# Routing of a sticky mixture of experts: packed keys, a triangle product and a carry product in place of VectorE steps, and a new order for the last tiles

## The chip, the cores and the metric

One Trainium2 chip, one core. The time is the device time of one execution in microseconds; lower is better. The engines are named as in the profile: PE is TensorE (PEld its weight loads), DVE is VectorE, ACT is ScalarE, POOL is GpSimd, SP is SyncE, whose queue issues most of the DMAs.

## The reference, cut to what matters

Three layers follow each other on 768 tokens of 512 columns: an attention in which a query sees only keys of its own hash bucket, a gated feed-forward layer with a 768 by 768 mixing of tokens (w_sg) and an output projection, and a mixture of 8 experts. The change lies in the choice of the expert in the third:

```python
logits = np.einsum('bsd,de->bse', x, w_gate)         # 768 x 8
local_gate = 1.0 / (1.0 + np.exp(-np.einsum('bsd,de->bse', x, w_local).squeeze(-1)))
prev_e = -1
for s in range(S):
    fresh_e = int(np.argmax(logits[b, s]))
    if s == 0 or local_gate[b, s] < 0.5:
        e = fresh_e
    else:
        e = prev_e if prev_e >= 0 else fresh_e
    prev_e = e
    p = softmax(logits[b, s])
    h = np.maximum(x[b, s] @ w1[e], 0.0)
    out[b, s] = p[e] * (h @ w2[e])
```

(The softmax and the loop's indices are abridged.) The choice is sticky: a token whose local gate is at or above one half takes the expert of the last token before it whose gate was below. It is thus a running "last update" over 768 tokens, then a count of how many tokens each expert has got so far.

## The kernel before, in words

Tokens are in 6 tiles of 128, one token per partition. The work runs in three stages: attention (8 heads), feed-forward with mixing, experts. In the second and third the order of the work is written out by hand: a text such as MIXING names one step after another ("mix 3 4", "out 5 6", "route 4", "gx 2 1"), the kernel records them in that order, and each engine executes its own instructions in the order in which they were recorded. An instruction that waits holds up all that stands behind it on its engine.

For each tile t of 128 tokens in MIXING: 18 products "mix" (PE, tile vs, 512 columns wide), the gating (DVE, g), 4 transposes (PE, gT), their rounding on ACT (gh) and the rest on DVE (gl), 12 products "out" (PE, tile o), the residual on DVE (x, L772). Then the routing of that tile, the generator route(t), whose steps are the "route t" of the text:

- 4 transposes of x (PE, x2T), a copy (ACT, x2t), the 9 logits (PE, lg): for tiles 0 to 4 in 32-wide column groups and a summing product, for tile 5 directly.
- DVE: the maximum of the 8 logits (rmx), whether the token updates (upd), the code of the maximal expert (sel, rw), the key of the token (key, L821): 8 times its position plus the code, or zero. ACT: the exponentials (ex, into the PSUM bank route_bank) with their sum se.
- PE transposes the key, spread over 128 columns (route_bank, L824; the last tile has a bank of its own, pk); DVE masks it with a triangle (km), takes the row maximum (pm), and the maximum with the tiles before (carry). Four DVE steps get the code out of the key (rf), two make the 8-wide choice in two types (ohb_all, oh_all).
- PE counts: products of the earlier tiles' choices with a matrix of ones, and of this tile's with a triangle (rk). DVE takes out the token's rank and its place (d), writes a 128 by 256 selection (pick, L863), a 128 by 128 one (slot, in gbc or cst), and ids and probabilities (what_all).

The selections are used at once: "gx" products gather the rows of the first two experts on PE out of the halves x2h (ACT) and x2l (POOL) of x, 8 products of 256 columns for each tile, and "fill" products gather the table of ids and probabilities. When the gx of tile 5 are done, the first expert's products (eh) start. In the expert stage PE multiplies by weights that arrive in 64 DMAs of 512 KB (raw, issued by SP); each is cast by ACT (w, L657) and its rest is formed by DVE or POOL (w, L663), which frees the buffer for the next DMA.

iota_p and rev_p (constants), the exponentials and the keys' product all lie in the one tile route_bank, and a reader or writer of any part of it waits for the last writer or readers of the tile.

Of the kernel before, what the change touches and what calls it, by code (L numbers as in the profile page):

```python
# [120 lines left out]
route 1, out 2 7, mix 4 10, gT 3, route 0, route 1, mix 4 11, route 1, out 2 8, out 2 9, wr 0, wh 0, wsg 5 1, wl 0,
mix 5 2, mix 4 12, route 1 *4, out 2 10, out 3 0, out 2 11, mix 4 13, res 2, route 1 *3, xd 2, mix 4 14,
route 1 *2, mix 5 3, wh 0, out 3 1, route 1, route 2, route 1, mix 4 15, out 3 2, wr 0, out 3 3, mix 4 16, out 3 4,
route 1, mix 4 17, out 3 5, wl 0, gated 4, mix 5 4, out 3 6, route 2, gl 3, mix 5 5, gT 4, mix 5 6, out 3 7,
out 3 8, route 2, out 3 9, route 1, out 3 10, out 3 11, wr 0, mix 5 7, route 1, mix 5 8, mix 5 9, route 2,
half 2 0, route 2 *2, out 4 0, mix 5 10, res 3, route 2 *2, mix 5 11, mix 5 12, mix 5 13, out 4 1, gl 4, route 2,
wh 0, route 2, mix 5 14, route 2, wr 0, out 4 2, mix 5 15, route 2, wh 0, mix 5 16, out 4 3, route 2, mix 5 17,
out 4 4, route 3, gated 5, route 2 *3, out 4 5, xd 0, route 2 *2, out 4 6, gT 5, route 2 *2, wl 0, route 3,
out 4 7, gl 5, out 5 0, wh 0, xd 1, out 4 8, route 3, out 4 9, route 3, out 4 10, route 2, out 4 11, out 5 1,
out 5 2, route 3, route 2, half 1 1, wl 0, half 2 1, route 3, res 4, route 3 *2, out 5 3, route 3 *3, out 5 4,  # L130
out 5 5, route 3, out 5 6, route 4, route 3, wr 0, out 5 7, out 5 8, route 3 *2, out 5 9, out 5 10, out 5 11,
route 3, res 5, xd 3, xd 5, route 3, wh 0, route 3, wr 0, route 3, xd 4, route 3, route 4, route 3, route 5,
route 4, route 5, route 4, route 3, gx 0 1, gx 0 0, gx 0 3, route 4 *2, half 4 0, half 5 0, route 5 *2, gx 1 0,
route 4, wl 0, half 3 0, route 5 *2, half 3 1, half 4 1, half 5 1, route 4, gx 0 2, route 4, wh 0, wr 0, route 4,
gx 1 1, fill 0, gx 1 3, route 4 *2, gx 1 2, route 5 *2, gx 2 1, gx 2 3, route 4 *3, wl 0, fill 1, gx 2 0, gx 2 2,
# [1121 lines left out]
```

## Time and profile before

| | before |
|---|---|
| median of 3 runs | 339.02 us (338.87 to 339.11) |
| the profiled execution | 338.87 us |
| its span | 336.9 us |
| PE busy | 325.5 us (97%), 1860 instructions |
| DVE busy | 264.8 us (79%), 504 instructions |
| ACT busy | 234.8 us (70%) |
| POOL busy | 203.9 us (61%) |

The span is what the profile shows of the core; 2.0 us of the execution's own time lie around it. Busy shares are of the span. Products on PE are pipelined: an entry lasts longer than the distance to the next one, so the distance between starts is what an instruction takes of PE's time.

### The profile page before, as it was taken

What the parts mean: (1) busy time and instruction counts of PE and PEld (TensorE: products, weight loads), DVE (VectorE), ACT (ScalarE), POOL (GpSimd) and SP (SyncE); (2) the same over time, 40 slices, a digit from 0 to 9 for tenths busy, and PEclk for the clock granted to TensorE, in tenths of its full rate; (3) what the DMA queues carried; (4) which work ended last, traced back from release to release, by engine and by line L of the source; (5) the groups of instructions that cost most, each with busy time, mean ns of one, the idle gap of its engine ahead of it and who ended that gap; (6) DMA issues with size and microseconds to landing.
All of it is one profiled execution on the core that took longest, in us unless ns stands there. A gap on an engine that the chain in (4) does not pass through costs nothing. (4 is left out here: it accounts for less than half of the span.)

```text
span 336.9 us, 5434 instructions
## 1 busy us (share of the span) xinstructions
PE 325.5 (97%) x1860; PEld 255.0 (76%) x1860; DVE 264.8 (79%) x504; ACT 234.8 (70%) x433; POOL 203.9 (61%) x162
## 2 busy tenths in 40 slices
PE   7899999999999999999999999999999999999994
PEld 6787786677678677688878777778878888788883
DVE  4899999998998884878864557888569877798970
ACT  3589888887988776288663455466659785978651
POOL 3378868587967745245734575949732683564652
PEclk9999999999999999999999999999999999999999
DMA  6914042214240115003014537456979979999711
GB/s 254 341 43 157 3 156 68 102 52 158 67 154 8 56 63 140 2 0 110 11 38 173 177 104 206 171 202 253 339 287 347 325 280 400 324 342 364 259 48 47
DMA packets 25952, 55.82 MB, mean 166 GB/s; under 512 B 2879, under 2 KB 7487, under 8 KB 25921
## 3 DMA queue, kind: packets, MB, share of 16 engines
q1 hardware_dynamic: 23872, 50.67, 42.7%
q0 software_dynamic: 1120, 3.15, 2.6%
q10 hardware_dynamic: 928, 1.62, 1.4%
q8 instruction: 16, 0.26, 0.3%
q14 instruction: 16, 0.12, 0.1%
HBM read 52.28 MB, written 3.67 MB: 166 GB/s over the span
## 5 line engine op out<-in xcount | busy, mean ns | idle before, releaser
L663 POOL TENSOR_TENSOR w<-raw,w 128x1024 fp32r<-128x1024 f32 x23 | 59.1, 2573 | 39.1 <-ACT w L657 38.0
L657 ACT CAST w<-raw 128x1024 fp32r<-128x1024 f32 x64 | 65.7, 1055 | 11.7 <-DMA raw<-in_w 9.2
L663 DVE TENSOR_TENSOR w<-raw,w 128x1024 fp32r<-128x1024 f32 x41 | 57.3, 1431 | 5.9 <-ACT w L657 5.8
L443 ACT COPY pt<-t 128x384 f32<-128x384 f32 x96 | 43.4, 485 | 11.9 <-PE t L437 11.7
L431 ACT ACTIVATE e<-s,nb_all 128x768 f32<-128x768 f32 x48 | 43.6, 910 | 10.4 <-DVE nb_all L427 9.8
L427 DVE TENSOR_REDUCE nb_all<-s 128x1 f32<-128x768 f32 x48 | 45.4, 952 | 5.7 <-PE s L423 5.4
L437 PE MATMUL t<-ident,e 128*128 128x128 f32 x288 | 42.4, 274 | 0.0
L437 PEld LDWEIGHTS t<-ident,e 128*128 128x128 f32 x288 | 34.3, 140 | 8.6 <-issue 2.3
L453 PE MATMUL po<-pt,vt 128*64 128x384 f32 x192 | 35.4, 497 | 0.0
L1048 PE MATMUL y<-w,hh 128*128 128x512 f32 (+1 forms) x144 | 34.6, 374 | 0.3 <-ACT hh L1032 0.3
L420 PE MATMUL s<-k,q 128*128 128x384 f32 x96 | 28.4, 377 | 0.8 <-ACT e L431 0.7
L1048 PEld LDWEIGHTS y<-w,hh 128*128 128x128 f32 x144 | 24.4, 189 | 4.9 <-ACT hh L1032 0.9
L746 PE MATMUL vs<-vn,wshi 128*128 128x512 f32 x72 | 25.6, 406 | 0.2
L423 PE MATMUL s<-k,q 76*128 76x384 f32 x96 | 25.0, 342 | 0.3 <-DVE q L411 0.3
L1015 PE MATMUL eh<-w,xh 128*128 128x512 f32 x96 | 25.0, 394 | 0.0
L392 POOL TENSOR_TENSOR k<-r,k 64x768 fp32r<-64x768 f32 x7 | 13.8, 1975 | 14.7 <-DVE k L382 9.4
L453 PEld LDWEIGHTS po<-pt,vt 128*64 128x64 f32 x192 | 12.0, 136 | 13.7 <-issue 13.4
L314 PE MATMUL h<-w_in_s,xTs 128*128 128x512 f32 x96 | 21.9, 389 | 0.0
L314 PEld LDWEIGHTS h<-w_in_s,xTs 128*128 128x128 f32 x96 | 18.0, 188 | 3.7
L1015 PEld LDWEIGHTS eh<-w,xh 128*128 128x128 f32 x96 | 17.7, 188 | 3.6
L420 PEld LDWEIGHTS s<-k,q 128*128 128x128 f32 x96 | 14.7, 190 | 7.2 <-ACT e L431 2.5
L273 POOL TENSOR_TENSOR cv_w<-cv_w,cv_a 128x512 f32<-128x512 f32 x11 | 14.3, 1304 | 7.3 <-DVE cv_w L285 7.2
(201 smaller groups left out, 726.4 us busy)
## 6 DMA issues: line engine op xcount, KB each, us to landing
raw<-in_w SPq DMA_DIRECT2D x64, 512.0 KB, 5.2
r<-in_qk SPq DMA_DIRECT2D x7, 768.0 KB, 4.5
raw<-in_w_in SPq DMA_DIRECT2D x8, 512.0 KB, 3.5
wsr<-in_w_sgT SPq DMA_DIRECT2D x6, 384.0 KB, 4.4
raw<-in_w_out SPq DMA_DIRECT2D x4, 512.0 KB, 3.7
vt<-in_v_tok ACTq DMA_DIRECT2D x1, 1536.0 KB, 7.2
xd<-x SPq DMA_DIRECT2D x6, 256.0 KB, 4.6
r<-in_qk SPq DMA_DIRECT2D x2, 384.0 KB, 4.0
```

The lines of the kernel that those rows point to most:

```text
L314: nc.tensor.matmul(ps, a[:, kc, ts_], w_in_s[:, b, kc, ns], start=(kc == 0 and i == 0), stop=(kc == 3 and i == 2))
L420: nc.tensor.matmul(s[:, j, :HALF], q1[:, ts_], k1[:, j * HALF:(j + 1) * HALF], start=True, stop=False)
L427: nc.vector.tensor_reduce(nb_all[:, h, t:t + 1], ss[h, t][:, :, :HALF], axis=AX.XY, op=ALU.max, negate=True)
L431: nc.scalar.activation(e, ss.pop((h, t))[:, :, :HALF], AF.Exp, bias=nb_all[:, h, t:t + 1], accum_out=rs_all[:, h, t:t + 1])
L437: nc.tensor.transpose(ps[:, i * P:(i + 1) * P], es[h, t][:, g, i * P:(i + 1) * P], ident)
L443: nc.scalar.copy(dst, tps.pop((h, t, g))[:, :HALF].rearrange("p (i q) -> p i q", i=3))
L453: nc.tensor.matmul(po[j * D:(j + 1) * D, :HALF], vt[:, kt, h * D:(h + 1) * D], pt[j][:, kt, :], start=(kt == 0), stop=(kt == NT - 1))
L657: nc.scalar.copy(slabs_of[i, e][:, 0, q * 2:(q + 1) * 2, :], raws[part])
L663: eng.tensor_tensor(hl[:, 1, q * 2:(q + 1) * 2, :], raws.pop(part), hl[:, 0, q * 2:(q + 1) * 2, :].bitcast(F32), op=ALU.subtract)
L746: nc.tensor.matmul(ps, a[:, kc, :], b[:, kc, :], start=(k == 0), stop=(k == 17))
L1015: nc.tensor.matmul(ps[e, n], a[:, kc, :], slabs_of[1, e][:, b, kc * 2 + n, :], start=(k == 0), stop=(k == 11))
L1048: nc.tensor.matmul(yb[part][:, cs], a[:, kc, :], slabs_of[2, e][:, b, kc, cs], start=(k == 0), stop=(k == 23))
```

## The change

The key is now one number whose bits hold the position and, in the lowest three, the expert (caps, made on the host: 8192 + 8 times the position + 7 - expert). The choice of the maximal expert's number from it stands in sel as before. In place of the transposed and masked key, DVE writes a diagonal matrix of the keys of updating tokens (kd), and PE multiplies it by the triangle; the last row's maximum of the tile before is spread over all partitions by a second product (ident's last column, spread, times pm of the tile before) into a 129th column, so that one row maximum (pm) does what the masking, the maximum and the carry did. One bit operation takes the code out (rf), one comparison makes the choice (ohb_all, bf16 alone). One more product with ones (code_b) adds 1024 times the code to the rank, so that the selection pick compares with that sum (pos) in one step; two small steps (place, rk) get the rank for slot. The negated maximum moves from DVE to ACT.

```diff
-            nc.vector.scalar_tensor_tensor(sel, lg[:, :NE], mx, cap_hi, op0=ALU.is_equal, op1=ALU.mult)
+            nc.vector.scalar_tensor_tensor(sel, lg[:, :NE], mx, caps[:, t, :], op0=ALU.is_equal, op1=ALU.mult)
             yield "sel"
             nmx = bp2.tile([P, 1], F32, tag="nmx", name="nmx")
-            nc.vector.tensor_scalar_mul(nmx, mx, -1.0)
+            nc.scalar.mul(nmx, mx, -1.0)
...
-            nc.vector.tensor_scalar(key, w, base_s[:, t:t + 1], upd, op0=ALU.add, op1=ALU.mult)
+            kd = bp2.tile([P, P], F32, tag="km", name="kd", bufs=1)
+            nc.vector.scalar_tensor_tensor(kd, ident, w, upd.to_broadcast([P, P]), op0=ALU.mult, op1=ALU.mult)
             yield "key"
-            pk = route_bank[:, :P] if t < NT - 1 else bank("t", f"pk{t}")[:, :P]
-            nc.tensor.transpose(pk, key.to_broadcast([P, P]), ident)
-            km = bp2.tile([P, P], F32, tag="km", name="km", bufs=1)
-            nc.vector.tensor_tensor(km, pk, tri, op=ALU.mult)
+            pk = route_bank[:, :P + 1] if t < NT - 1 else bank("t", f"pk{t}")[:, :P + 1]
+            nc.tensor.matmul(pk[:, :P], tri, kd, start=True, stop=True)
+            if t:
+                nc.tensor.matmul(pk[:, P:], ident[:, P - 1:].to_broadcast([P, P]), pms[t - 1], start=True, stop=True)
             yield "km"
-            nc.vector.reduce_max(pm, km, axis=AX.X)
+            pm = pms[t] = bp2.tile([P, 1], F32, tag="pm", name="pm")
+            nc.vector.reduce_max(pm, pk if t else pk[:, :P], axis=AX.X)
             yield "pm"
-            nc.vector.tensor_scalar(pm, pm, carry, None, op0=ALU.max)
-            yield "pm2"
             f = bp2.tile([P, 1], F32, tag="rf", name="rf")
-            nc.vector.tensor_scalar(f, pm, 0.125, MAGIC, op0=ALU.mult, op1=ALU.add)
-            if t < NT - 1:
-                nc.vector.reduce_max(cm, pk, axis=AX.X)
+            nc.vector.tensor_scalar(f.bitcast(U32), pm.bitcast(U32), 7 << 10, 0x46000000,
+                                    op0=ALU.bitwise_and, op1=ALU.bitwise_or)
             yield "f"
-            nc.vector.tensor_scalar(f, f, MAGIC, -8.0, op0=ALU.subtract, op1=ALU.mult)
-            if t < NT - 1:
-                nc.vector.tensor_scalar(carry, carry, cm, None, op0=ALU.max)
-            yield "f2"
-            nc.vector.tensor_scalar(ohb_all[:, t, :], rev_p, f, pm, op0=ALU.subtract, op1=ALU.is_equal)
-            yield "ohb"
-            nc.vector.tensor_scalar(f, f, pm, None, op0=ALU.add)
-            yield "f3"
+            oh = ohb_all[:, t, :]
             nc.vector.tensor_scalar(oh, rev_p, f, None, op0=ALU.is_equal)
             yield "oh"
...
-            for s in range(t + 1):
-                nc.tensor.matmul(pr, ones_b if s < t else tri_b, ohb_all[:, s, :], start=(s == 0), stop=(s == t))
+            for s in range(t):
+                nc.tensor.matmul(pr, ones_b, ohb_all[:, s, :], start=(s == 0), stop=False)
+            nc.tensor.matmul(pr, ones_b, code_b, start=(t == 0), stop=False)
+            nc.tensor.matmul(pr, tri_b, oh, start=False, stop=True)
...
-            nc.vector.tensor_scalar(d2[:, 0:1], f, -float(P), rank, op0=ALU.mult, op1=ALU.add)
-            nc.vector.tensor_scalar(d2[:, 2:3], rank, float(P) - 0.5, None, op0=ALU.is_lt)
-            yield "d"
-            nc.vector.tensor_scalar(pick, iota_p, d2[:, 0:1], d2[:, 2:3], op0=ALU.is_equal, op1=ALU.mult)
+            nc.vector.tensor_scalar(pick, iota_p, pos, None, op0=ALU.is_equal)
             picks[t] = pick
             yield "pick"
-            nc.vector.tensor_scalar(at_slot(t), iota_p[:, :P], 3.5 * P, rank, op0=ALU.add, op1=ALU.is_equal)
+            rank = rank_all[:, t:t + 1]
+            nc.vector.tensor_scalar(rank, f, BASE, STEP, op0=ALU.subtract, op1=ALU.mult)
+            yield "place"
+            nc.vector.tensor_scalar(rank, rank, pos, -1.0, op0=ALU.subtract, op1=ALU.mult)
+            yield "rk"
+            nc.vector.tensor_scalar(at_slot(t), iota_p[:, :P], 7 * STEP, rank, op0=ALU.subtract, op1=ALU.is_equal)
             yield "slot"
```

The host's constants change with it (small, consts), and one copy (code_b) is added to the step "tri" in the attention stage. In MIXING the "route" steps are fewer and stand elsewhere, and from "out 5 2" on the text is new; of its old and new last lines, these two show the kind of move:

```diff
-out 5 2, route 3, route 2, half 1 1, wl 0, half 2 1, route 3, res 4, route 3 *2, out 5 3, route 3 *3, out 5 4,
+out 5 2, route 3, route 2, half 1 1, half 3 0, wl 0, half 2 1, route 3, res 4, half 4 0,
+route 3 *2, out 5 3, route 3, out 5 4, out 5 5, route 3, out 5 6, route 4, wr 0, out 5 7, out 5 8, route 3, out 5 9,
```

What the new text makes of the engines' queues is shown at three places; digits behind a name are the tile and a buffer number. DVE, behind the residual of tile 5 (x<-o5). Before, from tile 3's slot (gbc) to the maximum of tile 5's logits (rmx<-lg5):

```order
L866 TENSOR_SCALAR gbc_1760<-route_bank_2035,rank_all_1742 128x128
L868 TENSOR_SCALAR se_2565<-se_2565 128x1
L870 TENSOR_SCALAR what_all_1743<-route_bank_2035,rf_2583,sm_73 128x8
L872 RECIPROCAL se_2565<-se_2565 128x1
L804 TENSOR_REDUCE rmx_2646<-lg4_2630 128x1
L806 TENSOR_TENSOR upd_2647<-lg4_2630,sm_73 128x1
L810 SCALAR_TENSOR_TENSOR sel_2651<-lg4_2630,rmx_2646,sm_73 128x8
L874 SCALAR_TENSOR_TENSOR what_all_1743<-route_bank_2035,se_2565,oh_all_1740 128x8
L813 TENSOR_SCALAR nmx_2665<-rmx_2646 128x1
L818 TENSOR_REDUCE rw_2652<-sel_2651 128x1
L821 TENSOR_SCALAR key_2670<-rw_2652,sm_73,upd_2647 128x1
L804 TENSOR_REDUCE rmx_2682<-lg5_2649 128x1
```

Now, from tile 4's diagonal of keys (kd) on:

```order
L819 SCALAR_TENSOR_TENSOR kd_2624<-ident_68,rw_2617,route_bank_2035 128x128
L802 TENSOR_REDUCE rmx_2640<-lg5_2611 128x1
L851 TENSOR_SCALAR rank_all_1742<-rf_2557 128x1
L853 TENSOR_SCALAR rank_all_1742<-rank_all_1742,pos_all_1740 128x1
L855 TENSOR_SCALAR gbc_1760<-route_bank_2035,rank_all_1742 128x128
L857 TENSOR_SCALAR se_2536<-se_2536 128x1
L859 TENSOR_SCALAR what_all_1743<-route_bank_2035,rf_2557,sm_73 128x8
L861 RECIPROCAL se_2536<-se_2536 128x1
L863 SCALAR_TENSOR_TENSOR what_all_1743<-route_bank_2035,se_2536,ohb_all_1741 128x8
L804 TENSOR_TENSOR route_bank_2035<-lg5_2611,sm_73 128x1
L808 SCALAR_TENSOR_TENSOR sel_2656<-lg5_2611,rmx_2640,cst_74 128x8
L827 TENSOR_REDUCE pm_2659<-route_bank_2035 128x1
```

The last steps of tile 3 stood ahead of tile 4's key; now they stand behind rmx<-lg5, and ahead of tile 4's row maximum (pm) and of tile 5's key, which is three rows below the last one shown.

PE at the same time, around tile 5's key product (pk5). Before:

```order
L912 MATMUL gx3_2658<-pick_2387,x2l1_2306 128x256
L912 MATMUL gx2_2657<-pick_2387,x2h1_2305 128x256
L912 MATMUL gx2_2657<-pick_2387,x2l1_2306 128x256
L824 MATMUL pk5_2731<-ident_68,key_2703 128x128
L912 MATMUL gx1_2656<-pick_2519,x2h2_2454 128x256
L912 MATMUL gx1_2656<-pick_2519,x2l2_2455 128x256
L912 MATMUL gx3_2658<-pick_2519,x2h2_2454 128x256
L912 MATMUL gx3_2658<-pick_2519,x2l2_2455 128x256
L853 LDWEIGHTS ones_b_77
L853 MATMUL rk4_2744<-ohb_all_1741,ones_b_77 128x8
```

Now:

```order
L901 MATMUL gx2_2628<-pick_2270,x2l0_2158 128x256
L901 MATMUL gx2_2628<-pick_2366,x2h1_2295 128x256
L901 MATMUL gx2_2628<-pick_2366,x2l1_2296 128x256
L822 MATMUL pk5_2681<-kd_2672,cst_74 128x128
L824 MATMUL pk5_2681<-pm_2659,ident_68 128x1
L839 LDWEIGHTS ones_b_76
L839 MATMUL rk4_2686<-ohb_all_1741,ones_b_76 128x8
L839 LDWEIGHTS ones_b_76
```

A key's product is now two instructions, one with the triangle (in cst), one with ident. Behind tile 5's stood 4 gx products ahead of the first of tile 4's count (rk4); now rk4 follows at once. Between the key products of tiles 4 and 5 stood 8 gx products and a table product; now there are 10 gx products, and tile 4's follows tile 5's logits (lg5) at once.

ACT, from tile 3's exponentials to those of tile 4. Before:

```order
L817 ACTIVATE route_bank_2035,se_2565<-lg3_2534,nmx_2563 128x8
L785 COPY x2t_2597<-x2T4_2592 128x512
L657 CAST w1_1_2545<-raw_2600 128x1024
L795 COPY lts_2635<-lg4_2630 128x128
L785 COPY x2t_2643<-x2T5_2638 128x512
L817 ACTIVATE route_bank_2035,se_2667<-lg4_2630,nmx_2665 128x8
L906 CAST x2h4_2672<-x_83 128x512
L906 CAST x2h5_2675<-x_83 128x512
L906 CAST x2h3_2695<-x_83 128x512
```

Now:

```order
L815 ACTIVATE route_bank_2035,se_2536<-lg3_2506,nmx_2534 128x8
L895 CAST x2h3_2541<-x_82 128x512
L895 CAST x2h4_2549<-x_82 128x512
L783 COPY x2t_2568<-x2T4_2563 128x512
L655 CAST w1_1_2517<-raw_2570 128x1024
L793 COPY lts_2601<-lg4_2596 128x128
L783 COPY x2t_2609<-x2T5_2604 128x512
L811 ACTIVATE nmx_2619<-rmx_2613 128x1
L815 ACTIVATE route_bank_2035,se_2621<-lg4_2596,nmx_2619 128x8
L895 CAST x2h5_2651<-x_82 128x512
```

The halves of tiles 3 and 4 (x2h3, x2h4), from which POOL forms x2l, are cast before tile 4's x2t; they stood behind tile 4's exponentials. The order on POOL and SP is the same in both.

## Rows read from the trace of the kernel before

**Rows 1.** The page: busy time, share of the span and instructions by engine
```profile
PE 325.5 (97%) x1860; PEld 255.0 (76%) x1860; DVE 264.8 (79%) x504; ACT 234.8 (70%) x433; POOL 203.9 (61%) x162
```

**Rows 2.** Busy time by stretch; the first row names the columns
```profile
core 0: us, PE busy (x) PEld busy (x) DVE busy (x) ACT busy (x) POOL busy (x), PEclk, DMA share, GB/s
174.00:212.00 38.00, 38.00 (x204) 29.53 (x205) 23.00 (x81) 19.64 (x35) 21.90 (x11) 1.00 0.50 161
216.00:221.50 5.50, 4.71 (x32) 2.98 (x32) 4.73 (x25) 2.34 (x6) 4.17 (x3) 1.00 0.00 0
221.50:232.00 10.50, 9.70 (x84) 9.25 (x85) 9.15 (x54) 5.46 (x13) 6.89 (x5) 1.00 0.80 302
...
250.00:320.00 70.00, 69.68 (x336) 57.42 (x335) 58.64 (x53) 55.46 (x70) 38.17 (x18) 1.00 0.90 323
```

**Rows 3.** Timeline of PE, a key's transpose: start, us, engine, line, operation
```profile
209.85 0.40 PE L746 MATMUL vs<-vn,wshi 128*128 128x512 f32 x1
210.09 0.27 PE L824 MATMUL route_bank<-ident,key 128*128 128x128 f32 x1
...
210.44 0.62 PE L746 MATMUL vs<-vn,wshi 128*128 128x512 f32 x2
```

**Rows 4.** Timeline of PE, a product of two f32 tiles in the attention stage
```profile
39.60 1.02 PE L508 MATMUL pvm<-vmean,ones_f 128*128 128x512 f32 x2
40.46 0.49 PE L437 MATMUL t<-ident,e 128*128 128x128 f32 x3
```

**Rows 5.** The chain of waits in order of time: start, us, what
```profile
222.26 0.81 PE gx L912 x6
223.07 0.87 PE lg L801 x8
```

**Rows 6.** Timeline of PE, tile 3's count and the product behind it
```profile
219.60 0.23 PE L853 MATMUL rk<-ohb_all,ones_b 128*128 128x8 bf16 x3
...
219.75 0.94 PE L769 MATMUL o<-w_out_s,gl 128*128 128x512 f32 x3
```

**Rows 7.** Timeline of PE, where it stood still in the tail
```profile
217.62 0.29 PE L824 MATMUL route_bank<-ident,key 128*128 128x128 f32 x1 [0.37 <-DVE key L821]
...
230.79 0.39 PE L912 MATMUL gx<-pick,x2h 128*128 128x256 f32 x1 [0.22 <-DVE pick L863]
```

**Rows 8.** Timeline of ACT, tile 5's copy and tile 4's exponentials
```profile
222.23 0.59 ACT L785 COPY x2t<-x2T 128x512 f32<-128x512 f32 x1 [0.79 <-PE x2T L783]
223.07 0.24 ACT L817 ACTIVATE route_bank<-lg,nmx 128x8 f32<-128x8 f32 x1 [0.25 <-DVE rw L818]
223.24 0.19 ACT L817 ACTIVATION_READ_ACCUMULATOR route_bank<-lg,nmx 128x1 f32 x1
```

**Rows 9.** Timeline of DVE, tile 3's last steps and tile 5's first
```profile
221.34 0.54 DVE L863 TENSOR_SCALAR pick<-route_bank,d 128x256 fp32r<-128x256 f32 x1
221.79 0.34 DVE L866 TENSOR_SCALAR gbc<-route_bank,rank_all 128x128 f32<-128x128 f32 x1
222.11 0.28 DVE L870 TENSOR_SCALAR what_all<-route_bank,rf,sm 128x8 f32<-128x8 f32 x1
...
223.96 0.17 DVE L804 TENSOR_REDUCE rmx<-lg 128x1 f32<-128x8 f32 x1 [0.61 <-PE lg L801]
...
225.06 0.28 DVE L830 TENSOR_REDUCE pm<-km 128x1 f32<-128x128 f32 x1
```

**Rows 10.** Timelines of ACT and PE in the expert stage, two late steps
```profile
246.01 1.06 ACT L657 CAST w<-raw 128x1024 fp32r<-128x1024 f32 x1 [1.07 <-DMA raw<-in_w]
...
247.60 0.66 PE L1026 MATMUL hT<-ident,hs 128*128 128x128 f32 x4 [0.38 <-ACT hs L1020]
...
294.21 1.19 PE L1048 MATMUL y<-w,hh 128*128 128x512 f32 x4 [0.32 <-ACT hh L1032]
```

**Rows 11.** Timeline of POOL, rests of x and of the weights
```profile
225.11 3.80 POOL L908 TENSOR_TENSOR x2l<-x,x2h 128x512 fp32r<-128x512 f32 x3 [4.94 <-issue]
228.86 4.75 POOL L663 TENSOR_TENSOR w<-raw,w 128x1024 fp32r<-128x1024 f32 x2
```

More of the change, by code (lines that the diff above doesn't have):

```diff
@@ L121 @@
[L121 to L125, printed above, removed]
@@ L131 @@
[L131 to L135, printed above, removed]
@@ new lines @@
+mix 2 16, out 1 7, mix 3 2, wl 0, mix 3 3, route 0 *3, out 1 8, wsg 4 2, mix 3 4, wr 0, mix 3 5, mix 2 17,
+out 1 9, mix 3 6, out 1 10, gated 2, wsg 4 0, mix 3 7, route 0, mix 3 8, gT 2, route 0, mix 4 0, wsg 4 1,
+mix 3 9, out 1 11, half 0 1, route 0, mix 3 10, wr 0, mix 3 11, out 2 0, out 2 1, mix 3 12, res 1, out 2 2,
+wsg 5 2, mix 3 13, wl 0, mix 4 1, out 2 3, mix 3 14, gl 2, route 1, mix 4 2, mix 4 3, out 2 4, route 0, wh 0,
+mix 3 15, mix 4 4, mix 3 16, route 0 *3, out 2 5, mix 3 17, mix 4 5, mix 4 6, wsg 5 0, route 1, route 0, wl 0,
@@ L139 @@
+fill 1, wh 0, wr 0 *2, gx 4 3, gx 4 2, gx 4 1, gx 4 0, fill 2, fill 3, gx 5 0, gx 5 2, gx 5 1, gx 5 3, route 4 *4,
+wr 0, route 5 *7, wl 0, wr 0 *3
 """
@@ L236 @@
     four = cst[:, 640:640 + NE + 1]
-    carry = cpool.tile([P, 1], F32, name="carry")
-    nc.vector.memset(carry, 0.0)
+    caps = cst[:, CAPS:CAPS + NT * NE].rearrange("p (t e) -> p t e", t=NT)
+    code_b = cpool.tile([P, NE], BF16, name="code_b")
     ones_b = cpool.tile([P, P], BF16, name="ones_b")
@@ L591, in side @@
                 nc.vector.tensor_copy(tri_b, tri_s)
+                nc.vector.tensor_copy(code_b, code)
             elif name == "sum_v":
@@ L613 @@
     pair = ctx.enter_context(tc.tile_pool(name="pair", bufs=2, reuse_waits="tile"))
-    oh_all = cpool.tile([P, NT, NE], F32, name="oh_all")
+    pos_all = cpool.tile([P, NT], F32, name="pos_all")
     ohb_all = cpool.tile([P, NT, NE], BF16, name="ohb_all")
@@ L802, in route @@
             mx = bp2.tile([P, 1], F32, tag="rmx", name="rmx")
-            upd = bp2.tile([P, 1], F32, tag="upd", name="upd")
+            upd = route_bank[:, P + 40 + t:P + 41 + t]
             nc.vector.reduce_max(mx, lg[:, :NE], axis=AX.X)
@@ L924 @@
         route_bank = bank("v", "route_bank")
-        rev_p, iota_p = route_bank[:, P:P + NE], route_bank[:, 2 * P:4 * P]
+        rev_p, iota_p = route_bank[:, P + 8:P + 8 + NE], route_bank[:, 2 * P:4 * P]
         nc.scalar.copy(rev_p, revc)
@@ L1214, in _consts @@
 def _consts(np, gate):
-    c = np.zeros((P, 640 + NE + 1), np.float32)
+    c = np.zeros((P, CAPS + NT * NE), np.float32)
     i = np.arange(P)
-    c[:, 0:128] = i[None, :] <= i[:, None]
+    c[:, 0:128] = i[:, None] <= i[None, :]
     c[:, 128:256] = i[:, None] < i[None, :]
-    c[:, 256:512] = np.arange(2 * P) - 3.5 * P
+    c[:, 256:384] = 7 * STEP + i
+    c[:, 384:512] = 6 * STEP + i
     for k in range(4):
         c[:, 512 + 32 * k:512 + 32 * k + NE + 1] = gate[k * P:(k + 1) * P]
-    c[:, 640:] = i[:, None] % 32 == np.arange(NE + 1)
+    c[:, 640:CAPS] = i[:, None] % 32 == np.arange(NE + 1)
+    for t in range(NT):
+        c[:, CAPS + NE * t:CAPS + NE * (t + 1)] = BASE + 8 * (t * P + i[:, None] + 1) + 7 - np.arange(NE)
     return c
```

55 lines of the change are left out of this document (25 added, 30 removed).

## The prediction, made before the changed kernel had run

> **What bounds the kernel now.** The page comes first: PE is busy for 97% of the span, DVE for 79% [rows 1]. So I look for the stretches in which PE is not the limit, with busy times by stretch [rows 2]. From 174 to 212 us, where the mixing runs and tiles 0 to 2 are routed, PE has no idle time, and it has next to none from 250 to 320. It is short of work only in the tail of the routing: 0.79 us of 5.5 and 0.80 of 10.5 (216 to 232), and there DVE is busy for 9.15 of 10.5 us in 54 instructions. The change takes work from DVE and gives some to PE. So two things must be priced: what PE gets where it is full, and what it is spared in the tail. The timeline of PE shows the waits of the tail, for the key and for the selection [rows 7]; the first expert's products follow the last gather at once, so what shifts the last gather (230.79 us) shifts the rest, but for the waits that PE still has later [rows 10].
>
> **What PE gets.** The order shows, for a tile: one transpose of the key becomes a product of two f32 tiles (triangle by kd), plus, but for tile 0, a carry product of one column, plus one bf16 product with ones (code_b). A product of two f32 tiles is two instructions in the trace, 0.86 us for 512 columns [rows 4], thus 0.43 each, and a quarter of that, 0.11, for 128. With 9 columns eight such instructions take 0.87 us [rows 5], again 0.11 each: below 128 columns a narrower one is not cheaper. The old transpose took 0.59 us less two 512-wide products of 0.235, thus 0.12, one instruction [rows 3]. So a tile gets 4 instructions for 1: 3 x 0.11 = 0.33 us more (tile 0: 0.11). Four bf16 products take 0.15 us [rows 6]; one more costs 0.03.
> - Tiles 0, 1, 2, where PE is full: 0.11 + 0.33 + 0.33 + 3 x 0.03 = **+0.86**. DVE and ACT are 61% and 52% busy there [rows 2]: the steps that DVE loses are worth nothing, and the negation that ACT gets (between nothing and the 0.24 us of a 128x8 exponential [rows 8]) is hidden. The same holds for the one copy (code_b) in the attention stage.
> - Tile 3: +0.36. PE waits for its key before [rows 7]; kd still waits for tile 3's exponentials, since both lie in route_bank, but these no longer wait for DVE's negation: I take 0.07 off. **+0.29**.
>
> Beside this row of 0.11 against 0.12 stands a rule that speaks against the change. The Trainium skill, "Perfetto Trace Analysis", section Transposes, says to transpose with the transpose operation and not with a standard matmul. Rows 3 and 4 agree: one instruction against two. Were the triangle product as cheap as the transpose, the sum would be 0.11 us smaller for each tile.
>
> **The tail, step by step**, on the clock of before (the shift of 1.15 us comes on top). Up to tile 5's logits the order is the same: the copy x2t of tile 5 ends at 222.82 [rows 8], the logits are there at 223.94 [rows 5, 9].
> - ACT negates tile 4's maximum behind that copy (0.24, estimated from rows 8), then the exponentials (0.24) and their sum, to about 223.40; kd follows. For kd, 128x128 with two inputs and two factors, the nearest row is the slot write, 0.34; the ends are the 128x128 maximum's 0.28 and the 256-wide pick's 0.54 [rows 9]. It ends at 223.75, when PE is in the last of its logits products (they end by 223.94), so PE goes on without a wait: 4 instructions to 224.25, then 10 gather products. Six took 0.81 with one changeover of 0.09 [rows 5], thus 0.12 each: to 225.5.
> - DVE stands at tile 5's maximum (rmx) until 223.96, as before [rows 9]. But behind it stand now the last steps of tile 3, which were done between 221.3 and 223 before: place and rank (0.15 and 0.21 by the pieces of tile 3's old steps, as an estimate), slot 0.34, ids 0.28 [rows 9], sum, reciprocal and probability, each starting before the end of the one ahead, about 1.3 us in all to 225.3. Then come tile 5's sel, tile 4's row maximum (0.28, from 225.55 to 225.84), and tile 5's key. That one waits for tile 5's exponentials, and these now wait for that row maximum, both being in route_bank: ACT 225.94 to 226.29, kd 226.33 to 226.67.
> - So PE stands from 225.5 to 226.7: **1.2 us**, as much as DVE's steps took before. From there it has in hand, before the last gather: the key product 0.44, tile 4's count 0.18, 8 gathers 0.96, a table 0.31 (two instructions and a changeover), 4 gathers 0.48, tile 5's count 0.21, 4 gathers 0.48, a table 0.31, 8 gathers 0.96, two tables 0.53: 4.86, thus 231.58. DVE has pick of tile 5 at 230.15, no longer late. Before, the last gather began at 230.79 [rows 7]: **+0.79**. DVE's gain is there (pick is 0.6 us earlier), but PE is now what is late.
>
> **What is taken back.** In the expert stage PE waits 0.38 us for hs, which stands on ACT behind a cast whose raw tile landed late, and 0.32 for hh [rows 10]. A PE that comes later by 1.9 us finds both done, unless the weights come later too. They should not: the halves of tiles 3 and 4 are now cast early on ACT, so POOL, which stood 4.94 us ahead of them [rows 11], is free for the two splits of 2.4 us (4.75 together) some 2 us sooner, and these free the buffers that SP's queue waits for. I take both: **-0.70**.
>
> **Sum**: 0.86 + 0.29 + 0.79 - 0.70 = +1.24 us on the profiled execution's 338.87 (span 336.9 and 2.0 around it): 340.1. The median of the runs lies 0.15 above that execution, so I forecast **340.2**. With kd at 0.54 and nothing taken back it is 340.2 + 0.7 + 2 x 0.2 = 341.3; with kd at 0.28 it is 340.1. About 0.2% (0.68 us) is what a measurement of this kernel can tell from no change, so faster means below 338.34 and slower above 339.70.
>
> **The rivals.**
> 1. *PE does not wait for tile 5's key* (not slower). If tile 3's small steps overlap more than I let them, or tile 5's logits come earlier, kd is ready by 225.5 and the 1.2 us go. Then the last gather comes at 231.58 - 1.2 = 230.4, 0.4 earlier than before, against 1.15 got earlier, and 0.70 is taken back: 339.0 or so, 338.6 if the waits of rows 10 are longer than the rows show. For it: DVE starts small steps well before the one ahead ends. Against it: steps that use the result of the one ahead don't. It decides from kd's end at 225.5.
> 2. *DVE's count of steps decides* (faster). By busy time a step of DVE is worth 9.15 / 54 = 0.17 us [rows 2]; 46 fewer in six tiles are about 15 in tiles 4 and 5: 2.6 us off the tail in place of 0.79 on it, 338.87 + 1.15 - 2.6 = 337.4. Against it: PE idles only 1.6 us there [rows 2], which caps it. The Trainium skill, "VectorE: DVE Perf Modes", section Rules for kernel authors, would have it so: it says to minimise the number of chained operations. Rows 2 bear that out for DVE alone.
> 3. *The carry product is nearly free* (faster). If its two instructions of one column start 0.03 apart like the bf16 ones [rows 6], 5 x 2 x 0.08 = 0.8 us go; with rival 1 that is 338.2. Against it: 9 columns cost as much as 128 [rows 5].
> 4. *Nothing is taken back*: the weights come as late as PE, 340.9 to 341.3. For it: SP's queue waits for splits on DVE, which begin behind the last gather.
>
> **Chances.** Forecast (339.7 to 340.6) 0.46; rival 4 0.14; rival 1 0.28; rivals 2 and 3 0.06 each. So faster 0.12, same 0.28, slower 0.60. A range from 338.6 to 341.3 leaves out rivals 2 and 3 and a little of the rest; the forecast's own is 339.7 to 340.6, and to 341.3 with rival 4, which has its sign.
>
> **What would show it.** DVE has about 46 instructions fewer, PE 22 more (6 + 10 + 6). Right: from 174 to 212 PE stays full and the same work ends 0.9 us later; in the tail DVE is far below 9.15 of 10.5; PE has one long wait, of about 1.2 us, ahead of tile 5's key product, and none for pick; the wait for hs near 247 is gone; POOL's split is earlier. Wrong: the last gather begins before 231 us; or the carry product's two instructions start less than 0.05 us apart; or PE waits more, not less, in the expert stage.

## The result, and the profile of the changed kernel

Forecast: 340.2 us, between 338.6 and 341.3, slower with a chance of 0.60. Measured: **340.68 us** (median of 19 runs, 339.55 to 342.98) against 338.32 for the kernel before, run in turns with it (19 runs, 337.59 to 340.47). The ratio is **1.0065** (95% interval 1.005 to 1.0081): slower, by some 2.2 us by the ratio where 1.24 had been forecast. The profiled execution of the change took 339.77 us (span 338.0), 0.9 more than the one of before. So two things have to be explained: where the 0.9 comes from, and why the medians lie further apart than the two profiles.

The page of the changed kernel, first line, and the busy time by stretch, with the columns of [rows 2]:

```profile
PE 327.0 (97%) x1882; PEld 256.9 (76%) x1882; DVE 260.0 (77%) x458; ACT 235.8 (70%) x439; POOL 203.8 (60%) x162
```

```profile
174.00:212.00 38.00, 38.00 (x208) 29.47 (x209) 19.50 (x60) 20.00 (x38) 21.10 (x11) 1.00 0.48 162
216.00:221.50 5.50, 5.16 (x30) 3.77 (x31) 3.40 (x16) 3.69 (x10) 5.50 (x4) 1.00 0.00 0
221.50:232.00 10.50, 8.71 (x85) 7.84 (x84) 7.15 (x38) 5.17 (x12) 7.90 (x5) 1.00 0.78 285
250.00:320.00 70.00, 70.00 (x338) 57.81 (x337) 59.59 (x53) 55.90 (x71) 38.92 (x17) 1.00 0.94 333
```

VectorE has 46 instructions fewer and PE 22 more. In the tail (221.5 to 232) DVE is busy for 7.15 us instead of 9.15 [rows 2], and PE for 8.71 instead of 9.70: the engine that lost the work is idler, and so is the one that was to profit.

PE's timeline, tile 2's key, where before one transpose stood [rows 3]:

```profile
210.56 0.39 PE L744 MATMUL vs<-vn,wshi 128*128 128x512 f32 x1
210.79 0.46 PE L822 MATMUL route_bank<-kd,cst 128*128 128x128 f32 x2
211.09 0.28 PE L824 MATMUL route_bank<-pm,ident 128*128 128x1 f32 x2
211.23 0.48 PE L744 MATMUL vs<-vn,wslo 128*128 128x512 f32 x1
211.55 0.39 PE L744 MATMUL vs<-vn,wshi 128*128 128x512 f32 x1
```

From the key's first instruction to the second "vs" behind it (starts) were 210.44 - 210.09 = 0.35 us, now 211.55 - 210.79 = 0.76: 0.41 more. The triangle takes 0.30, the carry product of one column 0.14.

PE's timeline in the tail, around tile 5's key product:

```profile
226.81 0.28 PE L901 MATMUL gx<-pick,x2l 128*128 128x256 f32 x1
228.46 0.46 PE L822 MATMUL pk<-kd,cst 128*128 128x128 f32 x2 [1.36 <-DVE ohb_all L834]
...
233.05 0.36 PE L901 MATMUL gx<-pick,x2h 128*128 128x256 f32 x1
...
234.09 1.19 PE L1004 MATMUL eh<-w,gxhi 128*128 128x512 f32 x4
```

Here is the long wait: 1.65 us from start to start, 0.12 of it the product's own. (The releaser named, ohb_all, ended 0.01 us before the product began, but the product reads kd, which ended 0.15 before.) There is no wait for pick any more. The last gather begins at 233.05 instead of 230.79 [rows 7]. DVE and ACT say why:

```profile
225.41 0.17 DVE L802 TENSOR_REDUCE rmx<-lg 128x1 f32<-128x8 f32 x1 [0.28 <-PE lg L799]
225.49 0.14 DVE L851 TENSOR_SCALAR rank_all<-rf 128x1 f32<-128x1 f32 x1
...
226.70 0.23 DVE L863 SCALAR_TENSOR_TENSOR what_all<-route_bank,se,ohb_all 128x8 f32<-128x8 f32 x1
226.96 0.17 DVE L804 TENSOR_TENSOR route_bank<-lg,sm 128x1 f32<-128x1 f32 x1
227.04 0.22 DVE L808 SCALAR_TENSOR_TENSOR sel<-lg,rmx,cst 128x8 f32<-128x8 f32 x1
227.17 0.28 DVE L827 TENSOR_REDUCE pm<-route_bank 128x1 f32<-128x129 f32 x1
...
227.96 0.35 DVE L819 SCALAR_TENSOR_TENSOR kd<-ident,rw,route_bank 128x128 f32<-128x128 f32 x1 [0.32 <-ACT route_bank L815]
```

```profile
225.61 0.20 ACT L811 ACTIVATE nmx<-rmx 128x1 f32<-128x1 f32 x1 [0.35 <-DVE rmx L802]
227.57 0.24 ACT L815 ACTIVATE route_bank<-lg,nmx 128x8 f32<-128x8 f32 x1 [1.76 <-DVE rw L816]
```

Between tile 5's maximum (225.41) and its flag (226.96) stand tile 3's seven steps, 1.47 us; then the exponentials wait on ACT until tile 4's row maximum (pm) has been read out of their bank, and kd waits for them. (The releaser named, rw, stands behind pm on DVE, and the exponentials do not read it.) In the expert stage PE waited for hs (the relu of an expert's first product, on ACT) and for hh (the rounding of its transpose, on ACT) [rows 10]. The same two places now, and POOL's splits of weights [rows 11]:

```profile
249.30 0.60 PE L1015 MATMUL hT<-ident,hs 128*128 128x128 f32 x4
...
295.37 1.20 PE L1037 MATMUL y<-w,hh 128*128 128x512 f32 x4
```

```profile
226.57 4.76 POOL L661 TENSOR_TENSOR w<-raw,w 128x1024 fp32r<-128x1024 f32 x2
```

The same product of hs now starts 1.70 us later than before (247.60), that of hh 1.16 (294.21), the end 1.1: half of the 2.26 us that the last gather came later is gone again, and PE shows no wait at either place. POOL's splits begin 2.3 us earlier than before (228.86).

### The profile page after: what moved, and what is told of

It reads as the page before. It is cut to its first block, busy times and chain, and to the rows that moved or that the text cites. A ratio compares the mean times of both kernels' runs of the same rounds, so it can differ in the third digit from the quotient of the medians.

```text
span 338.0 us, 5429 instructions
## 1 busy us (share of the span) xinstructions
PE 327.0 (97%) x1882; PEld 256.9 (76%) x1882; DVE 260.0 (77%) x458; ACT 235.8 (70%) x439; POOL 203.8 (60%) x162
## 5 line engine op out<-in xcount | busy, mean ns | idle before, releaser
L661 DVE TENSOR_TENSOR w<-raw,w 128x1024 fp32r<-128x1024 f32 x41 | 59.2, 1481 | 5.8 <-ACT w L655 5.7
```

The costliest lines, as they stand in the source:

```text
L661: eng.tensor_tensor(hl[:, 1, q * 2:(q + 1) * 2, :], raws.pop(part), hl[:, 0, q * 2:(q + 1) * 2, :].bitcast(F32), op=ALU.subtract)
```

## The experiments

The kernel before against itself (b0_again, below) gave 1.0011 (0.9995 to 1.0026): that is how far a ratio can be off here. Of the lines of MIXING the diffs below show the pieces that differ.

**Why the medians lie further apart than the profiles.** The changed kernel once more, without an edit:

> The changed kernel as it is, to see what lies between its profiled execution (339.77 us, +0.9 on the one of before) and its median (340.68, +2.4 on before's 338.32). Its 19 runs fall into two groups: about 339.5 to 340.8, and 341.5 to 343.0, and all of the second have a mean granted clock of 0.993 to 0.997, where most of the first have 0.998 to 1.0. Theory A (the clock): in some executions the clock falls to its lower level after PE's long stand of 1.64 us ahead of tile 5's key product; then runs above 341.3 are there again with a clock under 0.998, and a profile that falls into one of them shows a stretch of low clock that begins behind the stand. Theory B (the transfers): weights come late in some executions; then the clock is the same in all, and PE waits for casts of raw.

Measured: median 340.22 (339.55 to 342.91, 8 runs), ratio 1.0062 (1.0037 to 1.0087). The profile fell into the longest of these executions, 342.91 us. PE's tail and its granted clock (last figures but two):

```profile
229.87 0.46 PE L822 MATMUL pk<-kd,cst 128*128 128x128 f32 x2 [1.37 <-DVE ohb_all L834]
...
232.03 0.41 PE L901 MATMUL gx<-pick,x2h 128*128 128x256 f32 x1
```

```profile
228.00:231.80 3.80, 2.43 (x26) 2.26 (x25) 2.75 (x18) 2.35 (x4) 3.79 (x3) 1.00 1.03 416
231.80:235.20 3.40, 3.40 (x22) 3.31 (x22) 2.53 (x15) 0.00 (x0) 0.94 (x1) 0.50 1.04 422
235.20:239.00 3.80, 3.80 (x27) 3.36 (x27) 1.48 (x8) 2.54 (x6) 0.00 (x0) 0.99 0.33 124
```

Some 2 us behind the stand the clock is at its lower level, 1.2 GHz, for 3.4 us, though PE works throughout, and a gather product takes 0.21 us instead of 0.12: the start of the first expert's products is 2.9 us later than in the other profile of the change. Of these, 1.4 had been there since the start of the program, and 1.5 come from this stretch. The 1.4 arise before 14 us: DVE's first step waited for the DMA of sm (small constants) until 5.13 us instead of 4.26, and the first products (pj) were slow. They are shown for the change's first profile, then for this one, whose stretch follows with the columns of [rows 2]:

```profile
5.81 0.54 PE L401 MATMUL pj<-k,wz 128*66 128x384 f32 x2
```

```profile
6.67 1.86 PE L401 MATMUL pj<-k,wz 128*66 128x384 f32 x4 [1.00 <-DVE k L379]
```

```profile
5.70:10.00 4.30, 3.22 (x11) 2.32 (x12) 3.92 (x7) 1.58 (x2) 0.00 (x0) 1.00 0.58 224
```

The slow products start 0.32 us apart instead of 0.2, though the granted clock of that stretch reads 1.00 in both profiles; why is not shown. So theory A's stretch is there. Theory B's mark is not: behind 14 us PE waits for no cast of a raw tile. The late start is neither theory's. Nor does the mean clock tell the groups apart: all eight runs, the fast ones too, have 0.995 to 0.998. To weigh the stand, it is filled with needless products (the output does not depend on them):

```diff
+            elif name == "idle":
+                idle = bank("m", "idle")
+                for _ in range(t):
+                    nc.tensor.matmul(idle[:, :2 * P], hl[1][0][:, 2 * P:3 * P], picks[1], start=True, stop=True)
...
-gx 0 2, gx 1 2, route 5 *2, route 4,
+gx 0 2, gx 1 2, idle 12, route 5 *2, route 4,
```

> The changed kernel with 12 needless products of 256 columns put into PE's long stand (1.64 us), 0.12 us each, so 1.4 us: PE is busy there, and nothing on the path moves; the output is the same. Theory A (the clock falls because PE stands): the runs above 341.3 us are gone, all have a clock of 0.998 or more, the median is 339.6 to 339.9. Theory B (transfers, or anything else that does not hang on PE's being busy): the same two groups as the changed kernel, median 340.3 to 341.

Measured: 341.28 (339.59 to 343.42, 10 runs), ratio 1.0093 (1.0065 to 1.0122). Not lower, and 6 of 10 runs are above 341.2: theory A as the whole reason falls. Then the same with 6 products of 512 columns:

> The filled stand once more, with 6 products of 512 columns (0.235 us each, 1.41 in all) in place of 12 of 256. The profile of the change run again showed the clock at 1.2 GHz for 3.4 us right behind the stand, and 1.4 us lost there; but with 256-wide fillers the median was 341.28 and five of ten runs were above 341.3. [...] Theory C (the slow runs come from the start of the program, where the same profile has its first products 1.5 us late at the low clock): the same share of runs above 341.2 as with narrow fillers, and a profile that falls into one shows the start late and no low clock behind 20 us.

Measured: 340.51 (339.58 to 341.17, 6 runs), ratio 1.0059 (1.0039 to 1.0079). None of the six is above 341.2, where 6 of 10 were with the narrow products and 11 of 27 are of the unfilled change: on that count theory C failed. On its other mark it held: the profiled execution (341.08) has the first products 1.3 us late and the high clock in the whole tail. DVE's first step and the first products there:

```profile
4.46 0.17 DVE L328 TENSOR_SCALAR sm<-sm 128x12 f32<-128x12 f32 x1 [3.46 <-DMA sm<-in_small]
```

```profile
6.00 1.86 PE L401 MATMUL pj<-k,wz 128*66 128x384 f32 x4 [0.33 <-DVE k L379]
```

Here sm landed only 0.2 us later than in the change's first profile, so the products are slow without a late operand too, and, against theory C's words, at a granted clock of 1.00 (5.7 to 10 us). The lowest runs of the three (339.55, 339.59, 339.58) are the same: filling costs and gains nothing on the path. So the low clock behind the stand was seen in one profile and a late start in three, one of them of the kernel before (b0_again). Which of them sets the change's median, and how often each comes, these runs do not show.

**What PE got.** The key of tiles 0 to 3 transposed and masked again:

```diff
+            if t < 4:
...
+                nc.vector.tensor_scalar(key, w, upd, None, op0=ALU.mult)
...
+                nc.tensor.transpose(pk[:, :P], key.to_broadcast([P, P]), ident)
+                nc.vector.tensor_tensor(kd, pk[:, :P], tri_o, op=ALU.mult)
...
+                nc.vector.reduce_max(pm, kd, axis=AX.X)
+                if t:
+                    nc.vector.tensor_scalar(pm, pm, carry, None, op0=ALU.max)
...
+            else:
...
```

> The changed kernel with the key of tiles 0 to 3 transposed and masked on VectorE again (four VectorE steps more per tile, no triangle and no carry product on PE there); tiles 4 and 5, the order of the work and the long stand as in the change. PE-is-full: the starts of PE's instructions were shifted by 0.23, 0.45, 0.43 and 0.34 us in tiles 0 to 3; all but 0.03 of each goes: the first transpose of tile 5's x comes 1.3 us earlier, and the profiled execution is 338.4 to 339.0. Rival: VectorE's extra steps make tile 3's key or rank late, and less than half of the 1.3 us shows at the end. By theory A the second group of runs stays, as the stand does.

Measured: 338.26 (338.01 to 339.48, 12 runs), ratio 1.0003 (0.9987 to 1.0019). PE's timeline, tile 2's key and the stand:

```profile
210.15 0.27 PE L827 MATMUL route_bank<-ident,key 128*128 128x128 f32 x1
210.18 0.48 PE L746 MATMUL vs<-vn,wslo 128*128 128x512 f32 x1
...
226.90 0.46 PE L841 MATMUL pk<-kd,cst 128*128 128x128 f32 x2 [1.35 <-DVE ohb_all L851]
```

The stand is still there (1.35 idle), and yet the lowest run is 1.5 us below the change's, and the ratio that of no change. PE is past the transpose in 0.03 us; up to tile 5's transposes it is 1.56 us earlier than in the change (221.36 against 222.92), and the profile (338.53) is 1.24 shorter. By theory A the long runs should have stayed with the stand. They did not: the longest of these 12 is 1.5 us above the lowest, where 8 of the change's 19 are 1.9 or more above theirs. So the stand alone does not make them.

**What the stand costs.** First with another place for the flags and exponentials, and tile 3's last steps behind tile 5's key (for which rf gets three buffers):

```diff
-            upd = route_bank[:, P + 40 + t:P + 41 + t]
+            upd = bp2.tile([P, 1], F32, tag="upd", name="upd")
...
-            ex = route_bank[:, P + 16 + 8 * (t % 3):P + 24 + 8 * (t % 3)]
+            ex = bp2.tile([P, NE], F32, tag="ex", name="ex", bufs=3)
...
-gx 0 1, gx 0 0, gx 0 3, route 5, route 4, route 3 *7, half 5 0, half 5 1, route 5, route 4, gx 1 0,
+gx 0 1, gx 0 0, gx 0 3, route 5, route 4, half 5 0, half 5 1, route 5 *3, route 4, gx 1 0,
...
```

> The changed kernel without the long stand: exponentials and update flags lie in tiles of their own (not in the bank of the keys' product), and the last seven steps of tile 3 stand behind tile 5's key instead of ahead of it. My account of the tail (tile 5's key late because of these two): kd of tile 5 ends near 226.4 instead of 228.3, PE has no wait above 0.3 us ahead of tile 5's key product, the last gather comes some 1.3 to 1.6 us earlier, 0.3 to 0.7 of it lost again to later waits: the profiled execution 338.3 to 339.0, and no second group of runs by theory A. Rival: what is late is PE's own work or another step of DVE; then the wait only moves behind tile 5's key product, and the time stays within 0.4 us of 339.8.

Measured: 345.97 (343.27 to 347.67, 6 runs), ratio 1.023 (1.0186 to 1.0274). A miss, far outside both expectations. Timelines of DVE, POOL and PE:

```profile
218.28 0.90 DVE L863 SCALAR_TENSOR_TENSOR what_all<-ex,se,ohb_all 128x8 f32<-128x8 f32 x1
219.10 2.50 DVE L819 SCALAR_TENSOR_TENSOR kd<-ident,rw,upd 128x128 f32<-128x128 f32 x1
```

```profile
217.85 1.30 POOL L897 TENSOR_TENSOR x2l<-x,x2h 128x512 fp32r<-128x512 f32 x1
219.09 2.35 POOL L661 TENSOR_TENSOR w<-raw,w 128x1024 fp32r<-128x1024 f32 x1
```

```profile
221.65 0.49 PE L822 MATMUL route_bank<-kd,cst 128*128 128x128 f32 x2 [2.70 <-DVE kd L819]
```

The stand ahead of tile 5's key is gone, but kd of tile 3, 0.35 us long in the change, takes 2.50: to 221.60, just past the end of POOL's instruction beside it (221.44). So does the 8-wide what_all (0.90, to 219.18; POOL's ends at 219.15). Of the 12 kd and what_all of this profile, five are held like this, each to 0.03 to 0.16 us past the end of a tensor_tensor of POOL (1.58, 2.50 and 0.63; 0.90 and 2.11); the other seven, with POOL idle beside them, keep 0.35 and 0.21 to 0.23. So with both tensor operands in SBUF, VectorE's operation stood until POOL's was done. The Trainium skill, "SBUF — State Buffer", section Who interferes with whom, says that a VectorE instruction with two SBUF inputs contends with a GpSimd instruction that reads SBUF, and that this contention is an exclusive lock; the rows agree. PE stood 2.70 us, and the mean granted clock of these runs is 0.984 to 0.997, where the change had 0.993 to 1.0. What else makes these runs 346 us long is not shown. The next experiment leaves exponentials and flags in the bank and takes the order (and rf's buffers) alone:

> The changed kernel, and of the experiment without the stand only the order: tile 3's last seven steps stand behind tile 5's key, tile 4's row maximum too; exponentials and flags stay in the bank of the keys' product (in PSUM), because with all operands in SBUF the 128x128 kd took 2.50 us where POOL's tensor_tensor ran beside it, against 0.35. My account: kd takes 0.35 again, tile 5's exponentials wait for tile 4's key product alone, kd of tile 5 ends near 226.6, PE has no wait above 0.3 us ahead of tile 5's key product; the last gather comes 1.2 to 1.6 us earlier than in the change (233.05), the lowest run is 338.1 to 338.7, the median below 339.3. Rival (SBUF operands were not the cause of the 2.50 us): a long kd is there in this kernel too. Rival 2: the wait goes elsewhere in the tail, the lowest run stays within 0.4 of 339.55.

Measured: 339.15 (338.19 to 341.05, 12 runs), ratio 1.0029 (1.0011 to 1.0047). DVE, POOL and PE in its profile (where the program started 0.3 us later than in the change's):

```profile
218.48 0.34 DVE L819 SCALAR_TENSOR_TENSOR kd<-ident,rw,route_bank 128x128 f32<-128x128 f32 x1
...
226.91 0.35 DVE L819 SCALAR_TENSOR_TENSOR kd<-ident,rw,route_bank 128x128 f32<-128x128 f32 x1 [0.31 <-ACT route_bank L815]
```

```profile
217.58 1.30 POOL L897 TENSOR_TENSOR x2l<-x,x2h 128x512 fp32r<-128x512 f32 x1
```

```profile
227.09 0.28 PE L901 MATMUL gx<-pick,x2l 128*128 128x256 f32 x1
227.41 0.46 PE L822 MATMUL pk<-kd,cst 128*128 128x128 f32 x2
```

kd is 0.34 to 0.35 long again in all six tiles, at tile 3 with a tensor_tensor of POOL beside it from end to end: the place of its operand was the cause. So the bank that makes kd wait for the exponentials is also what keeps kd short. Tile 5's kd ends at 227.26 instead of 228.31, 1.3 us earlier if counted from the same start (0.4 later than expected); PE's wait falls from 1.5 to 0.2, and the lowest run by 1.36 us. The account of the tail holds.

**What was taken back.** The kernel before, unchanged, for a second profile:

> The kernel before, unchanged, for a second profile of it. The profiled execution that the prediction was made from took 338.87 us; most of its other runs took 337.6 to 338.4. Theory N: the 0.38 and 0.32 us that PE waited for hs and hh in that execution (raw tiles that landed late) are not there in the others, so there is little to take back, and the change costs the whole 1.45 + 0.80 us that the two traces show up to the first expert's products: then a profile of about 337.9 has no wait above 0.2 us for hs, and its last gather begins where it did (230.8). Rival: the waits are there in every execution, and the lower times come from the start of the program (the first products earlier or later); then the profile shows both waits again, and a first product of the attention at another time.

Measured: 338.67 (337.73 to 339.9, 12 runs). The profiled execution (339.62) had the late start (PE 1.9 us behind at the first scores, 1.5 in the tail), no wait for hs, and the wait for hh as before. Since the late start could have hidden the first, one more execution:

> The kernel before once more, one look. Its second profile had the start of the program 1.6 us late, no wait for hs, and the wait for hh as before; with the start taken off, its last product on PE came 0.8 us earlier than in the first profile. Theory N (the raw tile landed late in the first profiled execution by chance): no wait for hs above 0.2 us here either, and 337.5 to 338.2 us if the start is not late. Rival (a late start alone hides the wait): with a start as in the first profile the wait for hs near 247 is there again, and the time is 338.6 to 339.1.

Measured: 338.36, between the two ranges, with the start as in the first profile. ACT's timeline beside the first row of [rows 10]:

```profile
243.58 2.05 ACT L657 CAST w<-raw 128x1024 fp32r<-128x1024 f32 x2
245.53 0.59 ACT L1020 ACTIVATE hs<-eh 128x512 f32<-128x512 f32 x1
```

```profile
247.00 0.60 PE L1026 MATMUL hT<-ident,hs 128*128 128x128 f32 x4
...
293.76 1.19 PE L1048 MATMUL y<-w,hh 128*128 128x512 f32 x4 [0.32 <-ACT hh L1032]
```

Here the two casts follow each other; in the first profile the second began at 246.01, after 1.07 us of waiting for its raw tile. So the wait for hs was that execution's own, and the wait for hh is not. A last profile, in search of an execution without the latter:

> The kernel before a last time, one look. Its three profiled executions took 338.36, 338.87 and 339.62 us and all had PE wait for hh near 293 (0.48 us by distance of starts, two of them a further 0.05 to 0.25 for hs just ahead), while half of its runs take under 338.1. If those waits too are a matter of when the raw tiles land in an execution: a run of under 338.0 us has less than 0.2 us of them, and one of 338.3 or more has them again or a late start. If they belong to the kernel: they are there at any time, and what makes the fast runs fast is elsewhere (start or end of the program).

Measured: 338.51, wait for hh as before (0.33 us). No run below 338.36 has been profiled, so what the lower half of its runs lack stays open. Then the part of the change that was to take the waits back, alone:

```diff
-out 5 2, route 3, route 2, half 1 1, wl 0, half 2 1, route 3, res 4, route 3 *2,
+out 5 2, route 3, route 2, half 1 1, half 3 0, wl 0, half 2 1, route 3, res 4, half 4 0, route 3 *2,
...
```

> The kernel before with one part of the change alone: ACT casts the halves of tiles 3 and 4 where the change has it, ahead of tile 4's copy, so that POOL is done with them some 4 us earlier and its two splits of weights begin some 2 us earlier. The step of the prediction that took 0.70 us back rests on it. If the earlier splits take the wait back: PE's wait for hh near 293 (0.48 us by distance of starts in both profiles of before, 0.14 in the change) falls below 0.2, lowest run 337.1 to 337.4, ratio 0.998 to 0.9995. If only a later PE takes it back: the wait stays above 0.35, and the time is that of before, 1.000.

Measured: 338.01 (337.31 to 338.89, 12 runs), ratio 0.9988 (0.9974 to 1.0002). Its profile:

```profile
294.22 1.19 PE L1048 MATMUL y<-w,hh 128*128 128x512 f32 x4 [0.32 <-ACT hh L1032]
```

The wait for hh stays as it was. Earlier halves alone don't remove it; the gain that the median hints at is within what a ratio can be off. (POOL's splits did begin earlier, at 225.55.)

**A version that beats both.** Transposed keys for tiles 0 to 3, products for tiles 4 and 5, and the order without the stand:

> The new order of the experiment before this one together with transposed keys for tiles 0 to 3, whose median was 338.26 (lowest 338.01, ratio to before 1.0003) with the long stand still in it. If the two savings lie one behind the other on PE: lowest run 336.5 to 337.2, faster than before by 0.8 to 1.3 us. If later waits (weights that land no earlier) take the second saving: lowest run 337.5 to 338, ratio 0.998 to 1.001.

Measured: 337.31 (336.85 to 338.38, 12 runs), ratio 0.9978 (0.9965 to 0.9991): faster than before, by a little less than expected. One wait was left ahead of the tail, 0.43 us of idle PE for tile 5's residual. Two pairs of gathers are put there, and the later ones moved up:

```diff
-half 3 1, half 4 1, res 5, xd 3, xd 5, wh 0, wr 0, route 4, xd 4, route 5 *2,
-route 4 *4, gx 0 1, gx 0 0, gx 0 3, route 5, route 4,
+half 3 1, half 4 1, res 5, xd 3, xd 5, wh 0, wr 0, route 4, gx 0 1, gx 0 0, xd 4, route 5 *2,
+route 4 *4, gx 0 3, gx 1 1, gx 1 0, route 5, route 4,
...
```

> The version with transposed keys for tiles 0 to 3 and tile 3's last steps behind tile 5's key (median 337.31), and four gather products of tile 0 on PE ahead of tile 5's transposes, where PE waited 0.58 us for tile 5's residual; ten gather products stay between the two last keys. If PE's own work sets the tail: the last gather 0.4 to 0.6 us earlier, median 336.6 to 337.0. If VectorE's steps from tile 5's logits to pick set it: pick of tile 5 was there 1.2 us before its first gather, so less than that can't be lost; but weights that land no earlier could take it: 337.2 to 337.5.

Measured: **336.42** (336.24 to 336.74, 6 runs), ratio **0.9937** (0.9918 to 0.9957), 1.3% below the change (0.9937 / 1.0065 = 0.9873), and a little below the range expected. PE's timeline:

```profile
220.62 0.42 PE L793 MATMUL lg<-x2t,cst 128*32 128x128 f32 x8
220.97 0.39 PE L918 MATMUL gx<-pick,x2h 128*128 128x256 f32 x1
...
221.56 0.60 PE L783 MATMUL x2T<-ident,x 128*128 128x128 f32 x4
...
225.72 0.46 PE L841 MATMUL pk<-kd,cst 128*128 128x128 f32 x2
```

The transposes begin with no wait, and the last gather 0.4 us earlier, counted from the same start, than without the move. From there to the first expert's products the profile marks no wait on PE: its own work sets the tail now.

## Why the prediction was right, and where its sum was off

- **The sign and the place: right.** PE is full up to 212 us, so what VectorE lost there bought nothing (DVE busy 19.50 us instead of 23.00, PE 38.00 as before), and what PE gained cost its full length. The transposed version shows it from the other side: four tiles with VectorE's extra steps back are 1.5 us faster.
- **"The old transpose 0.12" was the mis-sized term.** The shift up to tile 5's maximum is 225.41 - 223.96 = 1.45 us [rows 9], where +0.86 and +0.29 had been forecast. The step took 0.59 less two products of 0.235 from [rows 3] for the transpose. But that rest is nearly all changeover to the next product, which stays: "vs" behind the key takes 0.32 with either kind of key, and the transpose 0.03 (210.15 to 210.18 in the transposed version). The triangle has 0.30 instead of 0.22, its first instruction taking 0.19 and its second 0.11. On the other side the carry product took 0.14 and not 0.22: its two instructions start 0.03 apart, the mark that was set for rival 3, and 0.11 pass to the next. So rival 3 is right about one of the two, and the triangle's 0.08 uses that up. The rule for transposes in the Trainium skill, "Perfetto Trace Analysis", section Transposes, points the same way, and the rows put the two forms further apart (0.03 against 0.30) than I had.
- **The tail: +0.79 forecast, 2.26 - 1.45 = 0.81 measured, by the mechanism named.** Tile 3's steps behind tile 5's maximum (1.3 forecast, 1.47 measured), the exponentials behind tile 4's row maximum, kd of 0.34 (0.35). The stand was 1.5 and not 1.2 us; PE's work behind it to the last gather 4.59 and not 4.86: two small errors that cancel. The reordered version removes both reasons and the wait with them; they were not taken apart.
- **"I take both: -0.70" came near by luck.** In the profiles 2.26 became 1.1, even more than forecast. But the wait for hs came from a raw tile that landed late in one execution of four; no change can take that back in the others. And POOL's earlier splits, on which the step rested, did come (226.57), yet alone they leave the wait for hh as it is. From the profile of before at 338.36 (no wait for hs) to the change's, both without a late start, 2.3 us at the last gather became 1.6 at the end (spans 338.0 and 336.4). The wait for hh is gone in the change and in the versions that come from it, but for 0.15 us in the one with narrow fillers; what removes it is not settled.
- **The sum**: 340.1 against 339.77 in the profile. The medians are 2.36 apart: the first profile of before (338.87) lies 0.55 above its median (338.32), in part through the late raw tile, and that of the change 0.91 below its own, for reasons left open above. The lowest runs, 339.55 and 337.59, are 2.0 apart, near the 2.26 that PE lost before anything was taken back. So rival 4, given a chance of 0.14, is what the medians look like, and the forecast's own case what the pair of profiles looks like: 340.68 lies just above the forecast's own 340.6. That 340.2 came so near is luck in part: its base, 339.02 from three runs, was 0.7 too long, and its cost of 1.24 some 1.1 too small.
- **Rival 2** (VectorE's count of steps) fell: DVE has 16 instructions and 2.0 us less in the tail, and PE waits longer. **Rival 1** is what the reordered version makes true: kd early enough, and the time 338.2 at its lowest.

## What to carry to other kernels

Price an instruction on a full engine by the distance between the starts on either side of it, with and without it, and count which changeover stays: a transpose that seemed to cost 0.12 us cost 0.03. Before steps are fused to save an engine, look which engine is waited for in that stretch; here the fused form cost more than it gave in tiles 0 to 3. That it pays in the last two is not shown: no version transposes those keys too in the new order. And take back a wait only if it stands in more than one profile.

## What was not expected of the hardware

- A 128x128 operation of VectorE took 2.50 us instead of 0.35 and a 128x8 one 0.90 and 2.11 instead of 0.23 beside POOL's tensor_tensor, when their tensor operands all lay in SBUF; with one of them in PSUM they kept their length beside the same work.
- After a stand of 1.5 us the granted clock was at 1.2 GHz in one execution for 3.4 us, and began to be so 2 us after PE had taken up work again. In the profiles without such a stretch (339.77 and, with transposed keys, 338.53) the stand was as long.
- One execution of a program was up to 1.9 us behind another at its first scores, some 10 us after its start: DVE's first operand landed between 4.26 and 5.13 us, and in three profiles the first products started 0.32 us apart instead of 0.2, at a granted clock of 1.00, in one of them with the operand there at 4.46.
